# Layer 1 of three early tiles computed transposed, in a kernel of block attention and routed experts

## The chip, the core and the metric

The kernel runs on one core of a Trainium2 chip. A core has TensorE (PE, with its weight loads shown apart as PEld), VectorE (DVE), ScalarE (ACT), GpSimd (POOL) and a queue engine (SP) that issues transfers. They run side by side and meet at semaphores; each takes its own instructions in the order in which the program wrote them. TensorE writes to a memory of its own, PSUM, from which VectorE and ScalarE read. A matmul there has a stationary operand, loaded by a LDWEIGHTS, and a moving one that is streamed past it. The metric is the device time of one execution in microseconds, as the median of several runs.

## The reference

```python
# attention in blocks of 64 tokens, batch 8, 8 heads, 576 tokens, head size 64
scores = scale * np.matmul(q_c, k_c.transpose(0, 1, 2, 4, 3))
attn = softmax(scores)                      # written out in the reference
x = heads of np.matmul(attn, v_c) side by side   # 4608 tokens x 512
# routing, token by token
e = argmax(logits[b, s]) if s == 0 or local_gate[b, s] < 0.5 else prev_e
p = softmax(logits[b, s])                   # over 8 experts
# expert: 512 -> 1024 -> 512
h = np.maximum(x[b, s] @ w1[e], 0.0)
out[b, s] = p[e] * (h @ w2[e])
```

## The kernel before

The first part, up to about 180 us, is the attention, in 18 pieces of 256 tokens. Its result goes to a table `x_d` in device memory, with nine router values a token. The second part runs the experts on tiles of 128 tokens that were sorted by expert. A tile is gathered from `x_d` through an index list, multiplied by `w1` (512 to 1024), put through a ReLU, multiplied by `w2` (1024 to 512), scaled by its probability and scattered to the output. Some 34 tiles run after the attention; which token goes to which tile is known only once the routing of all tokens is done.

Products are made of numbers split in two: `hi` is the value rounded to the format f32r, `lo` is the rest. A product takes three passes, hi x hi, hi x lo and lo x hi (`PASSES`). So every activation that enters a matmul is written twice: ScalarE writes `hi`, VectorE writes `lo` as the value less `hi`.

The tokens of expert 0 in the first half are known earlier. From them come three early tiles (0, 1 and 2), whose indices are ready during the attention. Their work fills TensorE while the attention drains and the routing of the rest is computed. This stretch is called the drain. For an early tile t its queues hold, in this order:

- `x`: four transposes of the gathered rows and their split into `xp` (hi and lo).
- `p`: the tile's probabilities, on VectorE with one exponential on ScalarE.
- `m`: layer 1. `mm1` keeps 128x128 of `xp` stationary and streams 512 columns of `w1` past it; the result `h` has tokens as rows, in one PSUM tile with the tag `sc`, of which there is one buffer. In four steps (one per 128 rows of `w1`) of six matmuls each; a fifth step is a ReLU on ScalarE from PSUM to `hsb` (L680).
- `h`: the result is needed with tokens as columns, since it is the stationary operand of layer 2. In two halves, `hp0` and `hp1`, each with four transposes of `hsb` into PSUM (L588), a `hi` on ScalarE (L590) and a `lo` on VectorE (L591). Each half has one buffer, so tile t's are written only after tile t-1's layer 2 has read them.
- `y`: layer 2, 24 matmuls into `y` (L641), then the scaling `ysb` on VectorE (L699) and the scatter on POOL (L700).

The order in the drain is written out by hand in `PAR["drain"]`, a list of queue names: each name takes the next step of its queue, and `*4` takes four. Other queues there are the last steps of the attention (`tx` transposes for the router, `ra` the router with L284, L289, L293 and L299), the routing of the second half (`rt`, `rk`, `of`, `oh`, `sl`, `ex`), the split of `w2` (`w`) and loads of weights. `play` (L456) goes through the list once, so the list sets the order on TensorE, VectorE and ScalarE alike. After the drain the loop over `step` runs the other tiles with `mm1`, `relu` and `h_parts` as before.

Of the kernel before, what the change touches and what calls it, by code (L numbers as in the profile page):

```python
# [8 lines left out]
F32 = mybir.dt.float32  # L9
# [4 lines left out]
AF = mybir.ActivationFunctionType  # L14
ALU = mybir.AluOpType
# [9 lines left out]
P = 128  # L25
# [15 lines left out]
        "q4 t1d*4 t1d p2*4 s0*4 s1*8 t2a*4 t2a t2b*4 t2b s1*4 o0*4 o0*4 o0 s1*2 t2c*4 o0 t2c t2d*4 t2d q5 p3*4 "  # L41
    ),
    "drain": (
# [8 lines left out]
    ),  # L52
    "p0": "AVPA",
    "p1": "PPPP",
# [11 lines left out]
def tile_attention_then_moe(ctx: ExitStack, tc, q, k, v, wg, wl, w1, w2, out):  # L66
    nc = tc.nc
# [21 lines left out]
    def load_w1(e, c):  # L89
        nc.sync.dma_start(raw1[c], w1[e, P * c:P * c + P, :])  # L90
# [17 lines left out]
    ps_s = ctx.enter_context(tc.tile_pool(name="ps_s", bufs=1, space=PSUM))  # L108
# [201 lines left out]
    V = nc.vector  # L310
    oh = pa1.tile([P, E, NT], BF16, name="oh")
# [7 lines left out]
    def trp():  # L319
        return ps_tr.tile([P, 512], F32, name="tr")  # L320
# [161 lines left out]
    with tc.manual_schedule(engines=MAN):  # L482
        def load(store, fn, i):
            def go():
                store[i] = fn(i)
            return lambda: [go]
# [43 lines left out]
    for b in range(B):  # L530
        t, p = divmod(b * S, P)
# [50 lines left out]
    def hilo_atoms(src_of, hi, lo):  # L582
        box = {}

        def tr():
            ps = box["ps"] = trp().rearrange("p (n t) -> p n t", n=4)
            for n in range(4):
                nc.tensor.transpose(ps[:, n], src_of(n), ident)  # L588

        return [tr, lambda: nc.scalar.copy(hi, box["ps"]),  # L590
                lambda: V.tensor_tensor(lo, box["ps"], hi.bitcast(F32), ALU.subtract)]  # L591
# [29 lines left out]
    PASSES = ((0, 0), (0, 1), (1, 0))  # L621
    W1, W2 = (w1h, w1l), (w2h, w2l)

    def mm1(xs, hs, c):
        for n, (a, w) in enumerate(PASSES):
            for j in range(2):
                nc.tensor.matmul(hs[:, j], xs[a][:, c], W1[w][c][:, 512 * j:512 * j + 512],  # L627
                                 start=(c == 0 and n == 0), stop=(c == 3 and n == 2))

    def mm1_upper(xf, hm):
        for c in range(4):
            for j in range(2):
                nc.tensor.matmul(hm[HT * j:HT * j + HT], xf[:, c], raw1[c][:, 512 * j:512 * j + 512],
                                 start=(c == 0), stop=(c == 3))
# [13 lines left out]
    def new_h():  # L650
        return ps_s.tile([P, 2, 512], F32, name="h", tag="sc"), pc.tile([P, F], F32, name="hsb", bufs=1)
# [27 lines left out]
    def relu(hsb, hs):  # L679
        nc.scalar.activation(hsb, hs.rearrange("p j f -> p (j f)"), AF.Relu)  # L680

    def part(name, late):
        if late is None:
            return pc.tile([P, 2, 4, P], F32R, name=name, bufs=1)
        return pa2.tile([P, 2, 4, P], F32R, name=name, tag=late, bufs=3 if late == "xs" else 2)
# [18 lines left out]
    xgs, xps, hps, prc, full, hsbs = {}, {}, {}, {}, {}, {}  # L704
# [5 lines left out]
    def early_x(t):  # L710
        xp = part("xp", None)
        xps[t] = xp[:, 0], xp[:, 1]
        return hilo_atoms(lambda n: xgs[t][:, P * n:P * n + P], *xps[t])
# [3 lines left out]
        return atoms  # L717

    def early_m1(t):
        hs, hsbs[t] = new_h()  # L720
        return [lambda c=c: mm1(xps[t], hs, c) for c in range(4)] + [lambda: relu(hsbs[t], hs)]

    def early_h(t):
        hps[t], atoms = [], []
        for g in range(2):
            hp = part(f"hp{g}", None)
            hps[t].append((hp[:, 0], hp[:, 1]))
            atoms += hilo_atoms(lambda n, g=g: hsbs[t][:, 512 * g + P * n:512 * g + P * n + P], *hps[t][g])
        return atoms

    def early_m2(t):
# [9 lines left out]
    sl = slots([pe2, pe2, pe2], 0, EARLY, ((0, TA),), qsA)  # L741
# [12 lines left out]
    for i in range(1, NS - 2):  # L754
# [12 lines left out]
        if 4 <= i < 12:  # L767
            c, col = divmod(i - 4, 2)
            col = slice(512 * col, 512 * col + 512)
            split(w1h[c][:, col], w1l[c][:, col], raw1[c][:, col])  # L770
    def w2_split(c):
        return [lambda: nc.scalar.copy(w2h[c], raw2[c]),
                lambda: V.tensor_tensor(w2l[c], raw2[c], w2h[c].bitcast(F32), ALU.subtract),
                lambda: load_w2(1, c)]


    n = NS - 1
# [23 lines left out]
    def gather_full(t):  # L801
        xgs[t] = gather(t, pc.tile([P, XR], F32, name="xg", bufs=4), x_d)
# [26 lines left out]
        s=lambda: sa, ld=load(vts, load_v, n), rt=lambda: sb, rk=sb_rank, of=lambda: offsets, oh=sb_onehots,  # L829
        sl=lambda: slots([pc, pc, pc], QB[1], QB[2], ((0, NT),), qs), ex=lambda: experts,  # L830
        g=lambda: [lambda t=t: gather_full(t) for t in (EARLY, EARLY + 1)],
        l1=lambda: [lambda c=c: load_w1(1, c) for c in range(4)],
        w=lambda: [f for c in range(4) for f in w2_split(c)],
        x3=lambda: early_x(EARLY))
# [5 lines left out]
    for k, fn in (("x", early_x), ("p", early_p), ("m", early_m1), ("h", early_h), ("y", early_m2)):  # L840
        for t in range(EARLY):
            queues[f"{k}{t}"] = lambda fn=fn, t=t: fn(t)
    play(PAR["drain"], queues)
    sl = slots([pa1, pc, pa2], QB[2], QB[3], ((0, TA), (TA, NT)), qs, [dict(tag=g) for g in ("v0", "v1")] + [dict(tag="pr", bufs=2)])
# [100 lines left out]
    with tc.manual_schedule(engines=MAN | {ET.SP, ET.Pool}):  # L945
# [3 lines left out]
        for t in range(EARLY, TMIN + 3):  # L949
            step(t, ok, mix)  # L950
            n = t - EARLY
# [28 lines left out]
```

## Time and profile before

| what | value |
|---|---|
| median of 3 runs | 726.73 us (725.91 to 727.65) |
| the profiled execution | 728.45 us |
| its span, first to last instruction | 726.7 us |
| mean granted TensorE clock | 0.974 |
| busy: PE, DVE, ACT, POOL | 659.7, 369.0, 270.7, 177.1 us |
| stretch of the early tiles, from the first matmul of layer 1 on | 183.5 to 228.8 us |

A row of a timeline reads: start in us, length in us, engine, line, operation, output <- input, shapes, count of merged instructions, and in brackets how long the engine was idle before it and what released it. A row of a group reads: line, engine, operation, shapes, count, then busy time and mean length in ns, then the idle time before it. A matmul's length is its latency, and matmuls overlap, so the distance between starts is what TensorE pays.

### The profile page before, as it was taken

What the parts mean: (1) busy time and instruction counts of PE and PEld (TensorE: products, weight loads), DVE (VectorE), ACT (ScalarE), POOL (GpSimd) and SP (SyncE); (2) the same over time, 40 slices, a digit from 0 to 9 for tenths busy, and PEclk for the clock granted to TensorE, in tenths of its full rate; (3) what the DMA queues carried; (4) which work ended last, traced back from release to release, by engine and by line L of the source; (5) the groups of instructions that cost most, each with busy time, mean ns of one, the idle gap of its engine ahead of it and who ended that gap; (6) DMA issues with size and microseconds to landing.
All of it is one profiled execution on the core that took longest, in us unless ns stands there. A gap on an engine that the chain in (4) does not pass through costs nothing. (4 is left out here: it accounts for less than half of the span.)

```text
span 726.7 us, 17109 instructions
## 1 busy us (share of the span) xinstructions
PE 659.7 (91%) x5594; PEld 523.6 (72%) x5594; DVE 369.0 (51%) x860; ACT 270.7 (37%) x432; POOL 177.1 (24%) x222
## 2 busy tenths in 40 slices
PE   4786878878999999999999999999999999999981
PEld 4665666666677788777888887778877888777861
DVE  2564655788685585356232563472586323454310
ACT  3564655656422234441222443422454222432210
POOL 3321222234022233223121231331243212231100
PEclk9998999999999999999999999999999999999986
DMA  9999999968723144145111352441276211234100
GB/s 211 207 211 275 257 241 236 272 144 191 229 89 118 46 161 141 57 142 173 33 48 43 95 171 83 147 156 47 90 240 221 75 47 35 89 121 140 40 29 15
DMA packets 102928, 97.49 MB, mean 134 GB/s; under 512 B 42672, under 2 KB 79536, under 8 KB 102768
## 3 DMA queue, kind: packets, MB, share of 16 engines
q1 hardware_dynamic: 96608, 75.70, 41.1%
q0 software_dynamic: 6160, 19.85, 8.3%
q8 instruction: 78, 1.28, 0.8%
q14 instruction: 82, 0.67, 0.3%
HBM read 76.48 MB, written 19.56 MB: 132 GB/s over the span
## 5 line engine op out<-in xcount | busy, mean ns | idle before, releaser
L641 PE MATMUL y<-w2h,hp 128*128 128x512 f32 x608 | 204.7, 407 | 9.8 <-DVE hp L591 6.2
L627 PE MATMUL h<-w1h,xp 128*128 128x512 f32 x608 | 178.3, 403 | 0.0
L641 PEld LDWEIGHTS y<-w2h,hp 128*128 128x128 f32 x608 | 115.8, 191 | 38.9 <-DVE hp L591 8.9
L627 PEld LDWEIGHTS h<-w1h,xp 128*128 128x128 f32 x608 | 111.4, 189 | 23.9 <-ACTq L861 0.2
L641 PE MATMUL y<-w2l,hp 128*128 128x512 f32 x304 | 121.9, 401 | 0.0
L700 POOL DMA_INDIRECT out<-ysb,sidx x38 | 41.1, 1082 | 274.3 <-DVEq L861 197.0
L627 PE MATMUL h<-w1l,xp 128*128 128x512 f32 x304 | 95.9, 397 | 0.0
L590 ACT CAST hp<-tr 128x512 fp32r<-128x512 f32 x76 | 41.2, 589 | 107.7 <-PE tr L588 100.7
L591 DVE TENSOR_TENSOR xp<-tr,xp 128x512 fp32r<-128x512 f32 x39 | 27.0, 691 | 104.6 <-ACTq L861 66.9
L699 DVE TENSOR_SCALAR ysb<-y,ppr 128x512 f32<-128x512 f32 x35 | 26.2, 748 | 94.2 <-PE y L641 81.7
L627 PEld LDWEIGHTS h<-w1l,xp 128*128 128x128 f32 x304 | 57.0, 188 | 14.7 <-DVEq L861 0.7
L641 PEld LDWEIGHTS y<-w2l,hp 128*128 128x128 f32 x304 | 58.2, 191 | 12.4
L680 ACT ACTIVATE hsb<-h 128x1024 f32<-128x1024 f32 x35 | 36.0, 1027 | 67.0 <-PE h L627 64.3
L591 DVE TENSOR_TENSOR hp<-tr,hp 128x512 fp32r<-128x512 f32 x76 | 49.3, 686 | 13.8 <-ACT hp L590 12.1
L613 ACT ACTIVATE pex<-pex 128x8 f32<-128x8 f32 x38 | 7.9, 209 | 119.8 <-DVE pex L612 119.8
L97 DVE TENSOR_TENSOR w1l<-raw,w1h 128x1024 fp32r<-128x1024 f32 (+1 forms) x29 | 40.9, 1428 | 22.9 <-ACT w1h L96 22.7
L594 POOL DMA_INDIRECT xg<-x_d,gidx x36 | 36.6, 1017 | 41.0 <-issue 24.4
L156 POOL COPY qr<-qt 128x512 f32<-128x512 f32 x34 | 20.0, 617 | 101.1 <-issue 71.3
L242 PE MATMUL o<-v,pT 64*64 64x65 f32 x1152 | 29.0, 232 | 16.4 <-DVE xs L256 12.6
L588 PE MATMUL tr<-ident,hsb 128*128 128x128 f32 x304 | 40.2, 273 | 0.3 <-ACT hsb L680 0.3
L242 PEld LDWEIGHTS o<-v,pT 64*64 64x64 f32 x1152 | 22.6, 140 | 24.8 <-DVE xs L256 15.2
L97 DVE TENSOR_TENSOR w2l<-raw,w2h 128x1024 fp32r<-128x1024 f32 x21 | 39.9, 1953 | 0.9 <-issue 0.9
(173 smaller groups left out, 832.9 us busy)
## 6 DMA issues: line engine op xcount, KB each, us to landing
raw<-in_moe_w SPq DMA_DIRECT2D x72, 512.0 KB, 4.6
x_d<-xs SPq DMA_DIRECT2D x18, 521.0 KB, 6.8
v<-in_v SPq DMA_DIRECT2D x72, 128.0 KB, 5.8
qt<-in_q SPq DMA_DIRECT2D x11, 512.0 KB, 6.5
kt<-in_k SPq DMA_DIRECT2D x11, 512.0 KB, 7.8
qt<-in_q SPq DMA_DIRECT2D x6, 256.0 KB, 6.3
kt<-in_k SPq DMA_DIRECT2D x6, 256.0 KB, 6.2
qt<-in_q SPq DMA_DIRECT2D x4, 384.0 KB, 6.1
```

Of the source, the lines that this page charges most:

```text
L97: (lo_eng or nc.vector).tensor_tensor(lo, raw, hi.bitcast(F32), ALU.subtract)
L156: eng.tensor_copy(dst, src)
L242: nc.tensor.matmul(o[64 * cp:64 * cp + 64, cc, DV * h:DV * h + D + 1], pT[64 * cc:64 * cc + 64, 4 * j + h, 64 * cp:64 * cp + 64], vt[64 * ...
L588: nc.tensor.transpose(ps[:, n], src_of(n), ident)
L590: return [tr, lambda: nc.scalar.copy(hi, box["ps"]), lambda: V.tensor_tensor(lo, box["ps"], hi.bitcast(F32), ALU.subtract)]
L591: lambda: V.tensor_tensor(lo, box["ps"], hi.bitcast(F32), ALU.subtract)]
L594: nc.gpsimd.indirect_dma_start(out=dst, out_offset=None, in_=src, in_offset=bass.IndirectOffsetOnAxis(ap=gidx[t].bitcast(U32), axis=0))
L627: nc.tensor.matmul(hs[:, j], xs[a][:, c], W1[w][c][:, 512 * j:512 * j + 512], start=(c == 0 and n == 0), stop=(c == 3 and n == 2))
L641: nc.tensor.matmul(y, hx[f // 4][a][:, f % 4], W2[w][c][:, f % 2, :], start=(f == 0 and n == 0), stop=(f == 7 and n == 2))
L680: nc.scalar.activation(hsb, hs.rearrange("p j f -> p (j f)"), AF.Relu)
L699: either(mix, lambda: V.tensor_scalar(ysb, y, pr, None, ALU.mult), lambda: y_mixed(ysb, y, ym, pr))
L700: nc.gpsimd.indirect_dma_start(out=out, out_offset=bass.IndirectOffsetOnAxis(ap=sidx[t].bitcast(U32), axis=0), in_=ysb, in_offset=None, bo ...
```

## The change

For the three early tiles alone, layer 1 is computed with the operands exchanged. `mm1_cols` keeps 128x128 of `w1` stationary and streams the 128 columns of `xp` past it. The result `hT` has the hidden units as rows and the tokens as columns, which is the form that layer 2 wants. It is the same sum over the same three passes: 96 matmuls of 128x128 per tile in place of 24 of 128x512. `hT` lies in the same single PSUM buffer (tag `sc`, same size). The transposes of `hsb` and the ReLU into `hsb` go. ScalarE writes `hi` as the ReLU of `hT` straight from PSUM, and VectorE writes `lo` as max(`hT`, 0) less `hi`, from PSUM too. In the list the six steps of `h` stand together: `h0` right behind the last step of `m0`, `h1` behind the last step of `y0` and ahead of the first steps of `m2`, `h2` behind the last step of `y1`. The other queues keep their order among themselves.

```diff
-    tx0 m0 ra1 x1 ra1 ra0*2 x1*2 h0 w h0 ra0 m1 ra0 h0 rt h0 p0 h0 rt m1 h0 rt
+    tx0 m0 h0*6 ra1 x1 ra1 ra0*2 x1*2 w ra0 m1 ra0 rt p0 rt m1 rt
...
+    def mm1_cols(xs, hT, f):
+        for c in range(4):
+            for n, (a, w) in enumerate(PASSES):
+                nc.tensor.matmul(hT[:, f // 4, f % 4], W1[w][c][:, P * f:P * f + P], xs[a][:, c],
+                                 start=(c == 0 and n == 0), stop=(c == 3 and n == 2))
...
     def early_m1(t):
-        hs, hsbs[t] = new_h()
-        return [lambda c=c: mm1(xps[t], hs, c) for c in range(4)] + [lambda: relu(hsbs[t], hs)]
+        hT = hsbs[t] = ps_s.tile([P, 2, 4, P], F32, name="hT", tag="sc")
+        return [lambda f=f: [mm1_cols(xps[t], hT, f + d) for d in range(2)] for f in range(0, 8, 2)] + [lambda: None]

     def early_h(t):
         hps[t], atoms = [], []
         for g in range(2):
             hp = part(f"hp{g}", None)
-            hps[t].append((hp[:, 0], hp[:, 1]))
-            atoms += hilo_atoms(lambda n, g=g: hsbs[t][:, 512 * g + P * n:512 * g + P * n + P], *hps[t][g])
+            hi, lo = hp[:, 0], hp[:, 1]
+            hps[t].append((hi, lo))
+            atoms += [
+                lambda: None,
+                lambda g=g, hi=hi: nc.scalar.activation(hi, hsbs[t][:, g], AF.Relu),
+                lambda g=g, hi=hi, lo=lo: V.scalar_tensor_tensor(
+                    lo, hsbs[t][:, g], 0.0, hi.bitcast(F32), ALU.max, ALU.subtract)]
         return atoms
```

TensorE, from the last matmuls of tile 0's layer 2 into layer 1 of tile 2, before:

```order
L641 MATMUL y<-w2h_81,hp_3324 128x512
L641 MATMUL y<-w2l_85,hp_3324 128x512
L641 MATMUL y<-w2h_81,hp_3324 128x512 x2
L641 MATMUL y<-w2l_85,hp_3324 128x512
L641 MATMUL y<-w2h_81,hp_3324 128x512
L627 MATMUL h<-w1h_70,xp 128x512 [waits Activation_49]
```

and now:

```order
L648 MATMUL y<-w2h_81,hp_3374 128x512 [waits Activation_49]
L648 MATMUL y<-w2l_85,hp_3374 128x512
L648 MATMUL y<-w2h_81,hp_3374 128x512 x2
L648 MATMUL y<-w2l_85,hp_3374 128x512
L648 MATMUL y<-w2h_81,hp_3374 128x512
L634 MATMUL hT<-xp,w1h_70 128x128 [waits DVE_49]
```

The first matmul of tile 2's layer 1 waited for ScalarE before, and waits for VectorE now.

VectorE, at the same place of the program: the one-hot rows of the routing (`rh`), the first step of the expert table (`te`), the scaling of tile 0 (`ysb`) and the low halves of tile 1 (`hp`). Before:

```order
L421 TENSOR_SCALAR rh<-iota_m,rq 128x128 x7
L591 TENSOR_TENSOR hp_3433<-tr,hp_3433 128x512
L812 TENSOR_TENSOR te_2986<-toff,iota_hp 128x368
L699 TENSOR_SCALAR ysb<-y,ppr 128x512
L564 COPY inv_3575<-tr 64x10 x2
```

and now:

```order
L421 TENSOR_SCALAR rh<-iota_m,rq 128x128 x7
L824 TENSOR_TENSOR te_2986<-toff,iota_hp 128x368
L706 TENSOR_SCALAR ysb<-y,ppr 128x512
L739 SCALAR_TENSOR_TENSOR hp_3640<-hT,hp_3640 128x512
L739 SCALAR_TENSOR_TENSOR hp_3641<-hT,hp_3641 128x512
L564 COPY inv_3732<-tr 64x10 x2
```

The first low half stood ahead of `te` and `ysb` and the second came later, behind the slot list; both now stand together behind `ysb`.

VectorE, between the end of tile 0's layer 1 and the start of tile 1's: the last split of `w2` (`w2l`) there, the router's reduction (L299) and copy (L289), the low part of tile 1's `x`. Before:

```order
L773 TENSOR_TENSOR w2l_84<-raw_2_92,w2h_80 128x1024
L299 TENSOR_REDUCE L<-lg 128x18
L301 COPY xs<-L 128x2x9
L289 COPY lT<-lg 128x256
L591 TENSOR_TENSOR xp<-tr,xp 128x512
```

and now:

```order
L785 TENSOR_TENSOR w2l_84<-raw_2_92,w2h_80 128x1024
L739 SCALAR_TENSOR_TENSOR hp_3373<-hT,hp_3373 128x512
L739 SCALAR_TENSOR_TENSOR hp_3374<-hT,hp_3374 128x512
L299 TENSOR_REDUCE L<-lg 128x18
L301 COPY xs<-L 128x2x9
L289 COPY lT<-lg 128x256
```

Tile 0's low halves moved ahead of the router's reduction.

16 rows, old and new, of the table PAR are left out of this document.

## The prediction

> **What bounds the kernel now.** I read the page's busy shares, then a window around the three early tiles, then the timelines of TensorE, VectorE and ScalarE in it. The columns of a window row are its length, then busy time (and count) of PE, PEld, DVE, ACT, POOL, granted clock, DMA share, GB/s.
>
> ```profile
> PE 659.7 (91%) x5594; PEld 523.6 (72%) x5594; DVE 369.0 (51%) x860; ACT 270.7 (37%) x432; POOL 177.1 (24%) x222
> 183.50:228.80 45.30, 44.24 (x353) 33.42 (x352) 34.88 (x130) 14.74 (x25) 8.06 (x10) 1.00 0.50 161
> 228.80:726.70 497.90, 473.75 (x2298) 375.59 (x2296) 225.73 (x457) 156.13 (x237) 115.13 (x93) 0.98 0.31 98
> ```
>
> The early tiles lie between 183.5 and 228.8 us. PE idles there 1.06 us of 45.3, and after it PE is busy for 473.75 of 497.9 us. So time that PE gains or loses in this stretch arrives at the end almost one to one; at most about 1 us of it can vanish into gaps. Three things of the stretch move: the matmuls of layer 1, the transposes of its result, and the point at which the PSUM tile of layer 1 comes free.
>
> **The new matmuls.** Each early tile now has 24 matmuls of 128x512; the change makes them 96 of 128x128, each with its own weight load.
>
> ```profile
> L627 PE MATMUL h<-w1h,xp 128*128 128x512 f32 x608 | 178.3, 403 | 0.0
> L627 PEld LDWEIGHTS h<-w1h,xp 128*128 128x128 f32 x608 | 111.4, 189 | 23.9 <-ACTq L861 0.2
> L588 PEld LDWEIGHTS tr<-ident,hsb 128*128 128x128 f32 x304 | 35.3, 141 | 6.8 <-ACT w2h L96 1.2 <-ACT hsb L680 0.8
> 230.66 1.08 PE L627 MATMUL h<-w1h,xp 128*128 128x512 f32 x4
> 231.59 0.64 PE L627 MATMUL h<-w1l,xp 128*128 128x512 f32 x2
> 198.03 0.30 PEld L627 LDWEIGHTS h<-w1h,xp 128*128 128x128 f32 x2
> 198.06 0.71 PE L627 MATMUL h<-w1h,xp 128*128 128x512 f32 x2
> 198.37 0.42 PEld L627 LDWEIGHTS h<-w1l,xp 128*128 128x128 f32 x2
> 225.21 1.04 PE L588 MATMUL tr<-ident,hsb 128*128 128x128 f32 x8
> 215.18 1.26 PE L559 MATMUL tr<-qv,rh 128*128 128x20 bf16 x36
> ```
>
> Durations are latencies and overlap; what counts is the distance of starts. Four matmuls from 230.66 to 231.59 stand 0.2325 us apart, so a tile's 24 take 5.58 us. A quarter of the columns at that rate would be 0.058 us each, and nothing would change (96 x 0.058 = 5.58). But a load has 128 columns as before, and it was hidden behind 512 moving columns. What a load costs uncovered is seen where a group starts and no matmul holds it up: the two loads from 198.03 fill 0.30 us, one lasts 0.188, so the second begins 0.112 after the first. The second matmul begins at 198.06 + 0.71 - 0.40 = 198.37, exactly where the third load begins: a load starts when the matmul before it starts. Hence a short matmul cannot follow faster than one load, 0.112 us. The nearest row of this shape, the transposes (128 loaded, 128 moving, a lighter load of 141 ns), goes at (1.04 - 0.273)/7 = 0.110. I take **0.112**. Bounds: 0.058 if loads hide after all; 0.170 if load and stream go one after the other (0.112 + 0.058); 0.2325 if 128 columns cost what 512 do. The pairs of L559, 0.031 apart, have 20 moving columns in bf16 and bound nothing here but the issue. 96 x 0.112 = 10.75, less 5.58, is +5.17 a tile, **+15.5 us** for three.
>
> [...]
>
> **The removed transposes.** Twenty-four go, in six groups of four.
>
> ```profile
> 199.54 0.60 PE L588 MATMUL tr<-ident,hsb 128*128 128x128 f32 x4
> 199.89 0.72 PE L627 MATMUL h<-w1h,xp 128*128 128x512 f32 x2
> 200.45 0.63 PE L627 MATMUL h<-w1l,xp 128*128 128x512 f32 x2
> 213.34 0.60 PE L588 MATMUL tr<-ident,hsb 128*128 128x128 f32 x4
> 213.69 0.72 PE L627 MATMUL h<-w1h,xp 128*128 128x512 f32 x2
> ```
>
> The second group of tile 0 takes 199.54 to 199.89 = 0.35 us, and the pair of matmuls behind it 0.56 where a pair otherwise takes 0.465: 0.45 us in all. The second group of tile 1 (213.34) gives the same: **-0.9 us** together. The other four groups lie at the waits below and are counted there.
>
> **Tile 0's parts now stand before the router on VectorE.** ReLU and split read PSUM directly, and the split's second half is put ahead of the router's reduction (L299).
>
> ```profile
> 195.37 1.07 ACT L154 COPY xT<-tr 128x512 f32<-128x512 f32 x2 [4.35 <-PE tr L164]
> 195.97 0.23 DVE L299 TENSOR_REDUCE L<-lg 128x18 f32<-128x72 f32 x1
> 196.50 0.64 PE L284 MATMUL lg<-xT,wg 128*32 128x256 f32 x8
> 197.43 0.66 PE L588 MATMUL tr<-ident,hsb 128*128 128x128 f32 x4 [0.29 <-ACT hsb L680]
> 225.90 1.07 ACT L590 CAST hp<-tr 128x512 fp32r<-128x512 f32 x2 [2.57 <-PE tr L588]
> 226.52 1.29 DVE L591 TENSOR_TENSOR hp<-tr,hp 128x512 fp32r<-128x512 f32 x2 [0.80 <-ACT hp L590]
> ```
>
> ScalarE is free at 196.44; two high halves from PSUM take 1.07 (to 197.5), and the second low half follows, about 0.7, to 198.2. Only then comes L299, before at 195.97, and its end releases the router's PSUM tile: the matmuls at 196.50 move to 198.2 + 0.23 + 0.05 = 198.45, +1.95. The transposes at 197.43 go and save about 0.25 there; the low part of tile 1's x, also behind on VectorE, costs 0.2 again. **+1.9 us**. Without that queueing it would be about -0.5.
>
> **Tile 2's layer 1 waits for tile 1's parts.** PSUM has one buffer for h. Before, the ReLU at 204.99 emptied it at once. Now it holds until tile 1's low halves are written, and these need buffers that tile 0's second layer still reads. On VectorE they stand behind everything queued there.
>
> ```profile
> 211.71 0.39 PE L641 MATMUL y<-w2h,hp 128*128 128x512 f32 x1
> 211.94 0.62 PE L627 MATMUL h<-w1h,xp 128*128 128x512 f32 x2
> 207.31 0.60 PE L588 MATMUL tr<-ident,hsb 128*128 128x128 f32 x4
> 204.99 1.03 ACT L680 ACTIVATE hsb<-h 128x1024 f32<-128x1024 f32 x1 [1.99 <-PE tr L372]
> 207.51 0.46 DVE L396 TENSOR_TENSOR_SCAN inc<-tr,zrow 128x144 f32<-128x144 f32 x1 [0.40 <-PE tr L391]
> 214.98 1.21 DVE L421 TENSOR_SCALAR rh<-iota_m,rq 128x128 bf16<-128x128 bf16 x7
> 216.12 0.68 DVE L591 TENSOR_TENSOR hp<-tr,hp 128x512 fp32r<-128x512 f32 x1
> 216.72 0.52 DVE L812 TENSOR_TENSOR te<-toff,iota_hp 128x368 f32<-128x368 f32 x1
> 217.17 0.74 DVE L699 TENSOR_SCALAR ysb<-y,ppr 128x512 f32<-128x512 f32 x1
> ```
>
> From 207.51 VectorE works without a gap; the clock of both engines there is PE's last routing matmul, so a later PE moves both alike. Counted in before's times: VectorE ends L421 at 216.12, te takes 0.45, ysb 0.66, the two low halves 0.60 + 0.69: 218.5. PE ends tile 0's second layer at 211.94, or 211.5 without the transposes at 207.31 (0.35 + 0.09). It then idles about 7 us, and tile 2 starts at 218.58 where it was 211.94: **+6.6 us**. Behind the waiting matmul stand the rest of tile 2, the slot matmuls (L559) and every later tile, so nothing overtakes it. The slot matmuls lead to the gather of tile 3, read by PE at 224.78 before (row below); from their end (216.4) that took 8.4 us at most, and now half of tile 2 (5.4 us) and tile 1's second layer (5.6) stand between, so the gather costs nothing. Nor does ScalarE, which does two instructions a tile where it did three.
>
> So long an idle time has a second price, visible at the end of the program:
>
> ```profile
> 703.33 0.77 PE L641 MATMUL y<-w2h,hp 128*128 128x512 f32 x1 [3.31 <-ACTq L861]
> 704.32 1.05 PE L641 MATMUL y<-w2h,hp 128*128 128x512 f32 x2
> 703.30:709.40 6.10, 6.07 (x14) 4.79 (x15) 0.00 (x0) 0.00 (x0) 0.00 (x0) 0.50 0.03 9
> ```
>
> After 3.31 us of idle PE the granted clock is 0.50 for 6.1 us; 14 matmuls take 0.43 each there in place of 0.23, and loads slow down too (4.79/15 = 319 ns). The same after 7 us: 14 x 0.2 = **+2.8 us**; zero if the clock stays up.
>
> **Tile 2's parts, before its second layer.**
>
> ```profile
> 224.78 0.60 PE L588 MATMUL tr<-ident,xg 128*128 128x128 f32 x4
> 226.54 0.50 PE L641 MATMUL y<-w2h,hp 128*128 128x512 f32 x1 [0.29 <-ACT hp L590]
> 227.44 0.73 PE L641 MATMUL y<-w2h,hp 128*128 128x512 f32 x2 [0.16 <-DVE hp L591]
> 224.98 0.75 DVE L699 TENSOR_SCALAR ysb<-y,ppr 128x512 f32<-128x512 f32 x1 [1.18 <-PE y L641]
> ```
>
> Here the eight transposes from 225.21 vanish. The y tile is free at 225.73 and the first low half written at 226.4, so the third matmul of the layer starts at 226.4 in place of 227.44: **-1.0 us**.
>
> Sum: 15.5 - 0.9 + 1.9 + 6.6 + 2.8 - 1.0 = **+24.9 us**. The profiled execution took 728.45 us (span 726.7 and 1.75 around it), so the sum gives 753.3; that execution is 1.7 above the median of 726.73, from which 24.9 gives **752 us**.
>
> **Rivals.**
>
> *Loads partly hidden.* If a load can start earlier than the row at 198.37 says, the distance lies between 0.058 and 0.112; at the middle, 0.085, the matmul term is 288 x 0.085 - 16.74 = +7.7 and the time 744. For it: loads of L559 run far closer than their length. Against it: loads and matmul starts coincide through the whole f32 stream. [...]
>
> *Load and stream in series, or a full-rate penalty for few columns.* At 0.170 the term is +32.2, the time 768. At 0.2325 (these rows never show fewer than 512 columns in this number format) it is +50.2, the time 786. Against both: the transposes go at 0.110 with a load and a stream of the same count.
>
> *The wait of tile 2 does not show*, since VectorE gets ahead while PE is slower: 752 - 6.6 - 2.8 = 743. Against it: VectorE's backlog begins only with L396, which PE releases last.
>
> *Not slower.* PE is cover in this stretch, and the routing chain, ending in tile 3's gather, sets when the steady tiles begin. Then added PE time costs nothing until it exceeds the chain's slack, and the time stays 727; it decides only if PE's idle time here were 25 us. The 1.06 us idle speaks against it.
>
> **How the numbers follow.** The forecast 0.56, its own range 748 to 758 (the distance up to 0.13, the clock term 0 or 2.8, the waits 1 us either way); loads hidden 0.13; series 0.10; full penalty 0.10; no wait of tile 2 0.07; not slower 0.04. The range 742 to 770 leaves out the penalty, the last case and the edge of the hidden loads. About 0.2% (1.5 us) can be told from no change; faster 0.02, same 0.02, slower 0.96.
>
> **What would show it.** In the changed profile: L634 matmuls 0.112 apart, or else the first term falls; an idle PE of about 7 us before tile 2's L634 group, released by VectorE's L739, with a granted clock of 0.50 behind it; the router matmul L284 before tile 1 about 2 us later against tile 0's end; steady tiles unchanged. If the steady tiles change length, the whole argument is wrong.

## The result, and the profile after

The changed kernel takes 775.51 us (median of 4 runs, 773.12 to 776.97) beside 727.19 of the kernel before: a ratio of 1.066, with a 95% interval of 1.064 to 1.069. It was forecast slower, at 752 us within 742 to 770. The direction held, the size did not: +48 us where +25 was forecast. Ratios leave out runs more than 1.5% above the fastest of their kernel; below, one run of four falls out in each of two kernels, so that their ratios are lower than their medians suggest.

From the page of the kernel after, the busy shares and the granted clock in 40 slices:

```profile
PE 689.7 (89%) x5786; PEld 557.9 (72%) x5786; DVE 368.4 (48%) x860; ACT 267.6 (35%) x429; POOL 177.4 (23%) x222
PEclk9989999999756599999999999999999999999986
```

The second row is the news. The same row of the page before:

```profile
PEclk9998999999999999999999999999999999999986
```

Before, the clock of TensorE read 8 or 9 tenths in all slices but the last; now it falls to 7, 5, 6 and 5 tenths in slices 11 to 14, 193 to 270 us. By windows of the same profile (length, busy time of PE, PEld, DVE, ACT, POOL, granted clock, DMA share, GB/s):

```profile
181.00:197.00 16.00, 16.00 (x223) 14.33 (x222) 8.53 (x23) 4.04 (x6) 0.00 (x0) 1.00 0.57 174
198.50:201.40 2.90, 0.02 (x1) 0.00 (x0) 1.57 (x4) 1.78 (x5) 0.00 (x0) 1.00 0.52 174
203.00:224.00 21.00, 21.00 (x102) 20.75 (x100) 4.73 (x20) 1.20 (x2) 0.00 (x0) 0.50 0.19 66
224.30:229.50 5.20, 5.20 (x17) 3.89 (x17) 1.67 (x8) 0.59 (x1) 0.00 (x0) 0.50 0.00 0
229.50:233.60 4.10, 4.10 (x17) 2.98 (x15) 3.86 (x18) 0.60 (x1) 1.10 (x2) 0.94 0.00 0
233.60:240.70 7.10, 0.06 (x2) 0.02 (x1) 6.31 (x23) 0.60 (x1) 3.88 (x6) 0.73 0.02 9
240.70:262.30 21.60, 21.60 (x133) 21.60 (x133) 4.87 (x26) 0.42 (x2) 2.27 (x2) 0.50 0.25 83
262.30:269.00 6.70, 6.70 (x20) 5.27 (x21) 0.00 (x0) 0.60 (x1) 0.00 (x0) 0.61 0.00 0
```

Read downwards: layer 1 of tile 0 at clock 1.00; an idle PE; layer 1 of tile 1, 21 us at clock 0.50 with PE busy throughout; layer 2 of tile 0, in which the clock comes back after 5.6 us; the second idle stretch; layer 1 of tile 2, again 21.6 us at 0.50; layer 2 of tile 1, in which it comes back after 5.3 us. The trace's record of the granted clock puts the first fall at 202.7 us, behind a wait of 2.94 and one of 0.54 us and just before tile 1's first matmul at 202.95, and the second at 236.8, inside the wait of 7.04. The timeline of PE shows what the clock does to a matmul:

```profile
181.15 0.28 PE L634 MATMUL hT<-xp,w1l 128*128 128x128 f32 x1
181.26 0.39 PE L634 MATMUL hT<-xp,w1h 128*128 128x128 f32 x2
181.48 0.28 PE L634 MATMUL hT<-xp,w1l 128*128 128x128 f32 x1
...
201.46 0.64 PE L284 MATMUL lg<-xT,wg 128*32 128x256 f32 x8 [2.94 <-DVE L L299]
202.63 0.67 PE L293 MATMUL lg<-ident,lT 128*128 128x128 f32 x2 [0.54 <-DVE lT L289]
...
203.20 0.41 PE L634 MATMUL hT<-xp,w1l 128*128 128x128 f32 x1
203.42 0.63 PE L634 MATMUL hT<-xp,w1h 128*128 128x128 f32 x2
203.84 0.41 PE L634 MATMUL hT<-xp,w1l 128*128 128x128 f32 x1
...
240.69 0.47 PE L634 MATMUL hT<-xp,w1h 128*128 128x128 f32 x1 [7.04 <-DVE hp L739]
```

In tile 0 three matmuls take 0.33 us, 0.111 each. In tile 1 three take 0.64, 0.213 each: the same matmul at 1.9 times the distance.

Set side by side, the stretch from the first matmul of layer 1 of tile 0 to the first of tile 3 (starts of the same matmuls in both traces, us):

| part | before | after | more | forecast |
|---|---|---|---|---|
| layer 1 of tile 0, to the transposes of tile 1's x | 12.23 | 16.92 | +4.7 | +5.2 |
| from there to layer 1 of tile 1 | 2.29 | 5.03 | +2.7 | +1.9 |
| layer 1 of tile 1 | 6.87 | 21.41 | +14.5 | +4.7 |
| layer 2 of tile 0 and the wait behind it | 7.01 | 16.33 | +9.3 | +6.6 |
| layer 1 of tile 2 | 7.24 | 21.60 | +14.4 | +7.5 |
| layer 2 of tile 1 | 5.60 | 8.04 | +2.4 | 0 |
| from there to tile 3 | 4.85 | 4.89 | 0.0 | -1.0 |
| sum | 46.1 | 94.2 | +48.1 | +24.9 |

The rest of the program is as long as it was: 497.1 us from there to the end before, 495.8 after. So the whole loss lies in this stretch, and the table says where.

### The profile page after: what moved, and what is told of

Its sections match the earlier page's. It is cut to its first block, busy times and chain, and to the rows that moved or that the text cites. A ratio compares the mean times of both kernels' runs of the same rounds, so it can differ in the third digit from the quotient of the medians.

```text
span 771.0 us, 17480 instructions
## 1 busy us (share of the span) xinstructions
PE 689.7 (89%) x5786; PEld 557.9 (72%) x5786; DVE 368.4 (48%) x860; ACT 267.6 (35%) x429; POOL 177.4 (23%) x222
## 5 line engine op out<-in xcount | busy, mean ns | idle before, releaser
L627 PE MATMUL h<-w1h,xp 128*128 128x512 f32 x560 | 162.5, 402 | 0.0
L627 PEld LDWEIGHTS h<-w1h,xp 128*128 128x128 f32 x560 | 103.0, 189 | 22.5 <-ACTq L873 0.2
L627 PE MATMUL h<-w1l,xp 128*128 128x512 f32 x280 | 88.2, 396 | 0.0
L590 ACT CAST hp<-tr 128x512 fp32r<-128x512 f32 x70 | 37.8, 589 | 97.7 <-PE tr L588 93.8
L648 PEld LDWEIGHTS y<-w2l,hp 128*128 128x128 f32 x304 | 58.7, 193 | 12.4
L627 PEld LDWEIGHTS h<-w1l,xp 128*128 128x128 f32 x280 | 52.5, 188 | 13.5 <-DVEq L873 0.4
L634 PE MATMUL hT<-xp,w1h 128*128 128x128 f32 x192 | 53.0, 370 | 7.0 <-DVE hp L739 7.0
L687 ACT ACTIVATE hsb<-h 128x1024 f32<-128x1024 f32 x32 | 32.9, 1027 | 65.4 <-PE h L627 64.9
L591 DVE TENSOR_TENSOR hp<-tr,hp 128x512 fp32r<-128x512 f32 x70 | 45.2, 685 | 12.6 <-ACT hp L590 10.8
L634 PEld LDWEIGHTS hT<-xp,w1h 128*128 128x128 f32 x192 | 45.5, 286 | 7.6 <-DVE hp L739 7.5
L242 PE MATMUL o<-v,pT 64*64 64x65 f32 x1152 | 27.8, 230 | 14.9 <-DVE xs L256 12.0
```

The lines of the kernel that those rows point to most:

```text
L242: nc.tensor.matmul(o[64 * cp:64 * cp + 64, cc, DV * h:DV * h + D + 1], pT[64 * cc:64 * cc + 64, 4 * j + h, 64 * cp:64 * cp + 64], vt[64 * ...
L590: return [tr, lambda: nc.scalar.copy(hi, box["ps"]), lambda: V.tensor_tensor(lo, box["ps"], hi.bitcast(F32), ALU.subtract)]
L634: nc.tensor.matmul(hT[:, f // 4, f % 4], W1[w][c][:, P * f:P * f + P], xs[a][:, c], start=(c == 0 and n == 0), stop=(c == 3 and n == 2))
L648: nc.tensor.matmul(y, hx[f // 4][a][:, f % 4], W2[w][c][:, f % 2, :], start=(f == 0 and n == 0), stop=(f == 7 and n == 2))
```

## The experiments

Theory 1 after the result: TensorE's clock falls in an idle stretch, and a stream of narrow matmuls, whose loads are not covered, does not bring it back. Theory 2: the narrow stream lowers the clock by itself. Theory 3: the exchanged operands cost, not the width. The stretch of the table above is given for each run (in its profiled execution, with the difference to the 46.1 of before), since the rest of the program varies between executions (493.9 to 497.2 us in these profiles). The half clock differs in it too: in the clock records of before and after, apart from the half clock in which both end, the rest of before is 497.1 us long with 10.2 us of it at clock 0.50 (545.6 to 549.0 and 702.7 to 709.5), that of after 495.8 with 6.8 (745.4 to 752.2). The medians of whole runs contain it and differ from the stretch by some microseconds. Times are medians of four runs; the kernel before took 729.51 beside the first four kernels and 729.47 beside the last three.

**Narrow matmuls alone.** Layer 1 of the early tiles stays as it was, in blocks of 128 columns of `w1`; a block of columns is now the outer loop.

```diff
+    def mm1_w(xs, hs, k, w_):
+        for i in range(256 * k, 256 * k + 256, w_):
+            for c in range(4):
+                for n, (a, w) in enumerate(PASSES):
+                    nc.tensor.matmul(hs[:, i // 512, i % 512:i % 512 + w_], xs[a][:, c], W1[w][c][:, i:i + w_],
+                                     start=(c == 0 and n == 0), stop=(c == 3 and n == 2))
...
-        return [lambda c=c: mm1(xps[t], hs, c) for c in range(4)] + [lambda: relu(hsbs[t], hs)]
+        return [lambda c=c: mm1_w(xps[t], hs, c, 128) for c in range(4)] + [lambda: relu(hsbs[t], hs)]
```

> The kernel before, with only the width of layer 1's matmuls changed for the three early tiles: xp stays stationary and w1 moving, as before, but in blocks of 128 columns (96 matmuls a tile in place of 24). Transposes, ReLU, order and buffers stay. Theory 1 (TensorE's granted clock falls in an idle stretch of some 3 us, and matmuls of 128 columns only fail to bring it back): no such idle stretch here, clock 1.00 throughout, matmuls 0.112 us apart, time before + 15.5 us, about 743. Theory 2 (a stream of 128-column matmuls pulls the clock down by itself): clock 0.50 somewhere in tiles 1 or 2, time before + 25 to 40, 752 to 767. Theory 3 (the cost is in w1 as the stationary operand, not in the width): time near before, 727 to 730.

Measured: 740.34 us (+10.8), ratio 1.016 (1.012 to 1.021), stretch 60.9 (+14.9). Two windows of this run, over layer 1 of tiles 1 and 2:

```profile
203.30:215.20 11.90, 11.74 (x107) 11.47 (x104) 6.25 (x22) 2.48 (x5) 0.00 (x0) 1.00 0.26 97
222.50:234.40 11.90, 11.90 (x137) 11.90 (x135) 10.77 (x44) 1.00 (x3) 6.38 (x8) 1.00 0.18 57
```

The clock is 1.00 through both. Theory 2 is out for tiles of this length, and so is theory 3: with `w1` moving as before the narrow matmuls alone cost in the stretch nearly what was forecast for them (+15.5). The whole run came out below the 743 expected; the rest of its profile, 493.9 us, is the shortest of all.

**The waits alone.** Matmuls and transposes of the kernel before, in the order of the change, with the PSUM tile of `h` kept, by a one-element read on VectorE, until the second low half is written.

```diff
         hs, hsbs[t] = new_h()
+        held[t] = hs
...
+        last = atoms[-1]
+        atoms[-1] = lambda: (last(), V.tensor_copy(hold, held[t][0:1, 0, 0:1]))
         return atoms
```

> The waits of the change without its matmuls: the kernel before with matmuls of 512 columns and its transposes, but the steps of h in the order of the change, and the PSUM tile of h held (by a one-element read on VectorE) until the second low half is written. Theory 1: PE idles 3 to 4 us before tile 1 and about 7 us before tile 2, the clock falls to 0.50 at both and comes back after 5 to 6 us of 512-column matmuls; time before + 10 for the waits + about 5 for the clock, 739 to 745. Theory 2: the clock falls in the same way, since the idle stretch is the same, so the two agree here; what the run tells is whether 512 columns bring the clock back within a tile. If they do not, both are wrong.

Measured: 738.57 us (+9.1), ratio 1.012 (1.009 to 1.016), stretch 58.4 (+12.4). The second wait is 6.1 us. The first fell apart into 1.71, 1.10 and 0.55 us, since the transposes of `hsb` run between, and there the clock did not fall (1.00 from 195 to 216 us); so the guess of two falls was wrong by one. From the waits of this run and its windows, the second:

```profile
222.87 1.19 PE L627 MATMUL h<-w1h,xp 128*128 128x512 f32 x2 [6.10 <-DVE hold L734]
```

```profile
222.80:227.80 5.00, 4.93 (x12) 3.84 (x12) 0.00 (x0) 0.00 (x0) 0.03 (x1) 0.52 0.14 52
227.80:231.70 3.90, 3.90 (x50) 3.28 (x49) 2.54 (x11) 0.00 (x0) 1.09 (x1) 1.00 0.02 4
```

With 512 columns the clock is back after 4.7 us, within the tile. In the first window 12 matmuls take 5.0 us where at 0.2325 each they would take 2.8: the wait costs 2.2 us through the clock, somewhat less than the 2.8 that the prediction had put on it.

**No idle time before the narrow stream.** The changed kernel, with matmuls added into the two waits.

```diff
-    m0 h0*6 ra1 x1 ra1 ra0*2
+    m0 h0*6 ra1 x1 ra1 f1 ra0*2
...
-    ex y0 h1*6 m2*2
+    ex y0 f2 h1*6 m2*2
...
+            for _ in range(n):      # n = 12 for f1, 29 for f2
+                nc.tensor.matmul(ps, w1h[0][:, 0:P], w1h[1][:, 0:512], start=True, stop=True)
```

> The changed kernel with matmuls added whose result nobody reads: 12 of 512 columns in the wait before tile 1 and 29 in the wait before tile 2, so that PE does not idle there; nothing is taken away. Theory 1: clock 1.00 through tiles 0 to 2, matmuls of layer 1 0.112 us apart in all three tiles, time 775.5 less the 24.6 us that the half clock cost, about 751. Theory 2: the clock falls all the same within the 10.7 us of tile 1, time 765 to 776.

Measured: 749.81 us (+20.3), ratio 1.028 (1.025 to 1.032), stretch 70.2 (+24.1). The windows over layer 1 of tiles 1 and 2:

```profile
203.70:215.10 11.40, 11.40 (x102) 11.14 (x102) 4.90 (x20) 1.20 (x2) 0.00 (x0) 1.00 0.23 85
229.80:241.50 11.70, 11.70 (x132) 11.70 (x133) 4.82 (x26) 0.42 (x2) 2.28 (x2) 1.00 0.18 54
```

41 matmuls more than the changed kernel, and a stretch that is 24.0 us shorter (25.7 by the medians). This is the cost of the half clock: the distances alone, 192 matmuls at 0.213 in place of 0.112, make 19.4 of it, and the rest lies in the second layers behind. What stays, +24.1, is the prediction's sum without its clock term (+22.1) within 2 us.

**Shorter waits.** The changed kernel in another order of the drain.

```diff
-    m0 h0*6 ra1 x1 ra1 ra0*2 x1*2 w ra0 m1
+    m0 ra1 x1 ra1 ra0*2 h0*6 x1*2 w ra0 m1
...
-    w rk*2 oh of*2 oh of oh of oh*5 sl oh*3 y0 oh*4 y0*2 oh*3 ex y0 h1*6 m2*2 sl
+    w rk*2 y0*3 h1*6 y0 m2*2 oh of*2 oh of oh of oh*5 sl oh*3 oh*4 oh*3 ex sl
```

> The changed kernel with another order in the drain: before tile 1 the router's steps stand ahead of tile 0's halves, and before tile 2 tile 1's halves stand right behind the ranks on VectorE, ahead of the scaling of tile 0, the one-hot rows and the expert table. The two waits should shrink to about 1.5 and 2 us, by queueing alone about 7 us less. Theory 1: both idle stretches are now under 3 us, so the clock stays at 1.00 and the half clock's 24.6 us go too; time about 744. Theory 2: only the queueing goes, time about 768.

Measured: 761.24 us, ratio 1.037 (1.033 to 1.042), stretch 83.4, the four runs spread from 754.8 to 768.9 with mean clocks of 0.958 down to 0.939. A miss for theory 1 as it stood. The waits did shrink, to 0.55 and 1.61 us before tile 1 and 1.41 before tile 2, yet the clock fell. The timeline of PE at the start of tile 1, and two windows:

```profile
203.43 0.30 PE L634 MATMUL hT<-xp,w1h 128*128 128x128 f32 x1 [1.61 <-DVE hp L739]
...
204.99 0.39 PE L634 MATMUL hT<-xp,w1h 128*128 128x128 f32 x2
205.21 0.36 PE L634 MATMUL hT<-xp,w1l 128*128 128x128 f32 x1
205.37 0.64 PE L634 MATMUL hT<-xp,w1h 128*128 128x128 f32 x2
```

```profile
203.40:205.50 2.10, 1.98 (x15) 1.86 (x16) 1.96 (x9) 0.00 (x0) 0.00 (x0) 0.94 0.18 70
205.50:223.70 18.20, 18.20 (x88) 17.83 (x87) 2.97 (x12) 1.20 (x2) 0.00 (x0) 0.50 0.17 51
```

The stream starts at full clock and loses it about 1.8 us later. No run shows a limit of 3 us, which was the author's estimate: here waits of 0.55 and 1.61 us stood ahead of a fall, and in the kernel before the clock went to 0.50 for 3.41 us at 545.64, just behind a wait of 1.80 us. Waits of 1.71, 1.10 and 0.55 us had no fall behind them in tile 1 of the next run. Theory 1 was amended: the narrow stream keeps the clock low once it has fallen.

**Waits and width together, at 128 and at 256 columns.** The two edits above in one kernel, with `w_` 128 and 256: the exchanged operands are not in it.

> The waits of the change and the narrow matmuls of the change, but not its transposed form: the kernel before in the order of the change with h held in PSUM until the second low half is written, and layer 1 of the early tiles in blocks of 128 columns of w1. From the first four runs, theory 1 amended: an idle stretch lowers the clock, and a 128-column stream with its loads uncovered keeps it low. Then tile 2 (6 us idle before it) runs at 0.50 to its end; its stretch from layer 1 of tile 0 to layer 1 of tile 3 is before's 46.1 + 12.4 (waits, from the run that had them alone) + 14.9 (narrow matmuls, from the run that had them alone) + about 9.7 (tile 2 at half clock) = 83, or 93 if tile 1 falls too; time 764 to 775. If the two parts only add up, the stretch is 73 and the time about 754.

> The same with blocks of 256 columns: 48 matmuls a tile, each with its own load. A load of 0.112 us fits under 256 columns (a half of 0.2325 is 0.116). Amended theory 1: matmuls stand about 0.12 apart, the array streams nearly all the time, so the clock comes back in tile 2 as it did with 512 columns; stretch 58.4 + 1 to 3 = 59 to 62, time 739 to 744. If the clock stays at 0.50 through tile 2, what matters is the number of loads or of instructions and not the share of time in which columns stream: stretch 68 to 72, time about 750.

Measured: 768.72 us with 128, ratio 1.052 (1.042 to 1.062), stretch 82.2; 740.06 us with 256, ratio 1.015 (1.011 to 1.020), stretch 58.6. Layer 1 of tile 2 and what follows in the run with 128:

```profile
232.30:253.90 21.60, 21.58 (x132) 21.60 (x133) 4.87 (x26) 0.42 (x2) 2.18 (x2) 0.50 0.25 87
253.90:257.60 3.70, 3.70 (x10) 2.93 (x11) 0.00 (x0) 1.03 (x1) 0.00 (x0) 0.50 0.00 0
```

Only tile 2 ran at half clock there. Ahead of tile 1 the run with 128 had waits of 1.71, 1.10 and 0.55 us with transposes between, and its narrow stream kept 1.00 through the tile:

```profile
202.74 1.09 PE L588 MATMUL tr<-ident,hsb 128*128 128x128 f32 x8 [1.71 <-ACT hsb L687]
206.90:218.50 11.60, 11.60 (x103) 11.26 (x103) 4.90 (x20) 1.21 (x2) 0.00 (x0) 1.00 0.23 86
```

The windows of the run with 256 from the start of tile 2, and its timeline of PE there:

```profile
223.20:228.60 5.40, 5.40 (x32) 5.31 (x33) 0.00 (x0) 0.00 (x0) 0.00 (x0) 0.50 0.14 52
228.60:232.00 3.40, 3.40 (x57) 3.40 (x54) 2.32 (x11) 0.00 (x0) 0.86 (x1) 0.94 0.00 0
```

```profile
223.65 0.63 PE L636 MATMUL h<-w1h,xp 128*128 128x256 f32 x2
224.07 0.41 PE L636 MATMUL h<-w1l,xp 128*128 128x256 f32 x1
224.28 0.63 PE L636 MATMUL h<-w1h,xp 128*128 128x256 f32 x2
...
229.66 0.40 PE L636 MATMUL h<-w1h,xp 128*128 128x256 f32 x2
229.90 0.28 PE L636 MATMUL h<-w1l,xp 128*128 128x256 f32 x1
230.02 0.40 PE L636 MATMUL h<-w1h,xp 128*128 128x256 f32 x2
```

In this pair the width alone differs, behind the same wait of 6.1 us. At half clock three matmuls with 256 columns take 0.63 us (223.65 to 224.28), as long as three with 128 (0.64). The two streams have the same rate of instructions and the same rate of loads, and PE is busy without a gap in both; they differ in how many columns pass in that time. With 256 columns the clock is back 5.9 us after the first matmul, with 512 after 4.7; with 128 it is not back after 21.6. At full clock the 256-column matmuls stand 0.12 apart (three in 0.36), and a tile costs next to nothing more than with 512: 58.6 against 58.4.

It is also the interplay in numbers: the waits alone +12.4, the narrow matmuls alone +14.9, together +36.1 and not +27.3 (by the medians +9.1, +10.8 and +39.3).

**The transposed form at its best.** The other order with added matmuls, 8 before tile 1 and 6 before tile 2.

> The changed kernel with the second order of the drain and with matmuls added whose result nobody reads in the two waits that were left (8 of 512 columns before tile 1, 6 before tile 2). Amended theory 1: without idle time ahead of it the narrow stream keeps clock 1.00, so time is before + 15.5 for the matmuls - 0.9 for the transposes + about 3 for the waits left, 744 to 748, and the spread of the runs of that order without added matmuls (755 to 769) goes. Theory 2 (the narrow stream lowers the clock by itself after some microseconds): 755 to 769 as before.

Measured: 744.63 us, ratio 1.021 (1.017 to 1.025), runs from 742.8 to 745.3, stretch 63.1 (+17.0). The windows over layer 1 of tiles 1 and 2:

```profile
205.30:216.70 11.40, 11.31 (x101) 11.03 (x100) 4.85 (x20) 1.21 (x2) 0.00 (x0) 1.00 0.13 48
225.10:236.90 11.80, 11.77 (x132) 11.77 (x133) 11.39 (x49) 0.42 (x2) 7.11 (x9) 1.00 0.18 57
```

Fourteen added matmuls give back 16.6 us of that order's median (13.1 if its longest run is left out), and the spread of its runs with them. What stays is mostly the price of the narrow matmuls: the transposed form at its best, as tried here, is 2.1% slower than the kernel before.

## Why the prediction had the direction right and the size wrong

**The new matmuls: right.** 0.112 us apart was read from two uncovered loads of the kernel before; at full clock they are 0.111 apart. +15.5 us was forecast, and the stretch grew by 14.9 where this part stood alone.

**The removed transposes: not measured alone.** The sums above fit with them, no more.

**Tile 0's parts before the router: the mechanism right, the size short.** The wait is where it was put, released by L299, but 2.94 us and then 0.54. The timelines of ScalarE and of VectorE say why:

```profile
198.48 0.61 ACT L738 ACTIVATE hp<-hT 128x512 fp32r<-128x512 f32 x1
199.85 0.60 ACT L738 ACTIVATE hp<-hT 128x512 fp32r<-128x512 f32 x1 [0.76 <-DVE hp L739]
```

```profile
199.13 0.69 DVE L739 SCALAR_TENSOR_TENSOR hp<-hT,hp 128x512 fp32r<-128x512 f32 x1 [2.41 <-ACT hp L738]
200.48 0.69 DVE L739 SCALAR_TENSOR_TENSOR hp<-hT,hp 128x512 fp32r<-128x512 f32 x1 [0.66 <-ACT hp L738]
201.09 0.22 DVE L299 TENSOR_REDUCE L<-lg 128x18 f32<-128x72 f32 x1
```

The prediction let ScalarE write both high halves at once, as it does from two PSUM tiles. Now ScalarE waited for VectorE between them: four steps in a row where it counted three. Both halves now come from one PSUM tile; that this is the cause was not shown, since no run splits it.

**Tile 2's wait: the place right, the size by luck.** 7.04 us, released by L739, where about 7 was forecast. Two errors cancel in it. Counted from the last routing matmul (L391, at 207.24 before and 228.47 now), TensorE was done with the layer 5.0 us later where 4.3 was counted, since the layer began at half clock, and tile 2 started 12.2 later where 11.3 was counted, since ScalarE and VectorE took turns here too:

```profile
239.94 0.69 DVE L739 SCALAR_TENSOR_TENSOR hp<-hT,hp 128x512 fp32r<-128x512 f32 x1 [0.72 <-ACT hp L738]
```

**The price of the idle time: the step that failed.** The prediction took the end of the kernel before, where 14 matmuls ran at clock 0.50 after a wait, and put 2.8 us on the second wait. That row was one of 512 columns. The step assumed that the narrow stream would bring the clock back within some 6 us as the wide one did, and it put no price on the first wait. The runs showed both assumptions false: the clock fell before tile 1 too, behind waits of 2.94 and 0.54 us, and with 128 columns it stayed at half through all of both tiles. The term measured 24.0 us (the changed kernel against the one with its waits filled), not 2.8. With it the sum of the prediction's own terms, 22.1 + 24.0, is 46.1 of the 48.1 found.

**Tile 2's parts, before its second layer: half right.** The third matmul of that layer starts 2.00 us after tile 1's second layer instead of 2.66; the gain does not show in the table's last part because three more matmuls of the layer now stand ahead of tile 3.

**The rivals.** None of them described what happened. The full penalty for few columns came near in size (786) and for a wrong reason: its 0.2325 us a matmul is close to the 0.213 found in tiles 1 and 2, but those come from the half clock, and in tile 0 the same matmul took 0.111.

## What to carry to other kernels

Before narrowing a matmul's moving side, compare the distance of two uncovered weight loads with the distance of the matmuls: here 256 columns (0.12 us apart) still covered a load of 0.112 us and 128 (0.111 apart, where a quarter of 0.2325 would be 0.058) did not, and the removed transposes did not pay for that. The narrow stream was also fragile in its clock here: it ran at 1.00 where waits of at most 1.1 us stood right ahead of it, but behind waits of 0.55 and 1.61 us it fell to 0.50 in one run and stayed there to the end of the tile's stream. Where such a wait cannot be removed, wide matmuls that nobody reads, put into it, can be cheap: 41 of them were worth 24 us here.

## What the runs showed of the hardware that was not expected

- The same stream held either clock. In the runs with narrow matmuls alone and with added matmuls the 128-column stream kept 1.00 through whole tiles (11 to 12 us) when it came in at 1.00 with at most 1.1 us of idle time right ahead of it, and in the changed kernel (both tiles) and the run with waits and 128 columns (tile 2) it kept 0.50 for over 21 us when it came in at 0.50.
- PE's busy time did not decide the clock's return: 128 and 256 columns gave the same distance of 0.213 us at half clock and a busy PE throughout, and only with 256 did the clock return, after 5.9 us. The two differ in the columns that pass in a microsecond: with 128 columns these are 128/0.112 = 1143 at full clock and 128/0.213 = 601 at half clock, with 256 columns at half clock 1202. What the clock goes by was not shown. Few columns alone did not bring a fall: in the run with waits and 128 columns only 13 transposes of 128 columns began between 200.1 and 203.5 us, about 490 columns a microsecond, and the clock stayed at 1.00.
- The half clock came in steps. In the clock records of the traces before and after every stretch at 0.50, but for the one that outlasts the program (12.4 and 14.3 us), is a whole multiple of 3.41 us long: 3.41 or 6.83 before; 3.41, 6.83, 27.3 or 30.7 after. Whether it matters where a wait falls among these steps was not tested.
- How short the gap must be is not settled. Ahead of tile 1, waits of 1.71, 1.10 and 0.55 us with transposes between left the clock alone in the run with waits and 128 columns, and so did 1.1 us ahead of tile 2 in the run with added matmuls; 1.41 us, and 0.55 and 1.61 us, in the other order did not. The spread of that order's runs (754.8 to 768.9 us, mean clocks 0.958 to 0.939) suggests that the same gaps do not always have the same effect.
